# Regrouping batch 1's attention and moving its q^T to a DMA transpose in a fused attention and expert kernel

## The chip, the cores and the metric

The kernel runs on one core of a Trainium2 chip. The metric is device time in microseconds (us) of one execution. A profile records one execution with every instruction and every DMA packet; its times count from the start of the span, which is some 2 us shorter than the device time (330.9 and 332.65 us for the profiled run of the kernel before). Engines: PE is TensorE, PEld its weight loads, DVE is VectorE, ACT is ScalarE, POOL is GpSimd, SP is SyncE.

## The reference

Eight batches of attention with 8 heads, sequence 1024 and head size 64, in which k and v are first projected from 1024 to 64 positions; then a layer with two input matrices, a maximum and an output matrix.

```python
k_proj = einsum('ks,bhsd->bhkd', E, k);  v_proj = einsum('ks,bhsd->bhkd', F, v)
attn   = softmax(q @ k_proj^T / sqrt(64)) @ v_proj          # (8, 8, 1024, 64)
x      = attn, transposed and reshaped to (8192, 512)
out    = maximum(x @ w1, x @ w2) @ w_out                    # (8192, 512) float32
```

## The kernel before

The loads cast q, k and v of one batch to fp16, 1 MB each, and are issued by GpSimd. A batch has four attention "groups" (g, j): four heads g and half of the positions j. A group is a score step (TensorE, then exp on ScalarE), a sum step, a value step, and a multiply on VectorE. The projected k is transposed too; that tile is called kpt. The layer that follows works in 16 "units", two to a batch; each unit's products are cut into small pieces, between which the steps of later batches are put by hand. Unit (1, 0) needs only the groups with j = 0 of batch 1, unit (1, 1) those with j = 1.

The scores need q transposed. There are two ways to do it:

```python
def step_qt(t, h0, nh=2, i0=0, i1=NI, att=False):      # TensorE, then a copy by VectorE
    ...
            nc.tensor.transpose(out=qt_ps[...], in_=t["q"][:, h0 + h, ...], identity=ident16)
    nc.vector.tensor_copy(out=t["qt"][...], in_=qt_ps[...])

def step_qt_dma(t, h0=0, h1=H):                        # a DMA transpose, issued by SP
    nc.sync.dma_start_transpose(out=t["qt"][:, h0:h1]..., in_=t["q"][:, h0:h1]...)

def step_gate(t, n="kpt"):                             # GpSimd waits here until t[n] is written
    nc.gpsimd.tensor_copy(out=junk, in_=t[n][0:1, H - 1, 0:1])
```

GpSimd works in order, so a gate holds back all loads behind it. In the kernel before, batches 2 to 7 use the DMA transposes, with the next batch's loads behind a gate. Batch 1 transposes on TensorE, and all its four groups run within unit 0. Batch 2's k is loaded directly behind batch 1's q; its v and q follow as soon as batch 1's projection has freed their buffers.

The softmax here doesn't subtract the row's maximum and nothing guards it: scores larger than these inputs give would overflow.

Of the kernel before, what the change touches and what calls it, by code (L numbers as in the profile page):

```python
# [16 lines left out]
def kernel(  # L17
# [14 lines left out]
    B, H, S, D = q.shape  # L32
# [27 lines left out]
    def mm_bank(dtype=FP32, n=None):  # L60
        if n is None:
            n = turn.pop(0)
            turn.append(n)
        return ps.tile([128, 512 if dtype == FP32 else 1024], dtype, tag=f"mm{n}", name="mm_ps")

    def att_banks(dtype=FP32):
        return ps.tile(
            [128, 2, 512 if dtype == FP32 else 1024], dtype, tag="att", bufs=2, name="att_ps"
        )
# [6 lines left out]
            name=nc.get_next_instruction_name(),  # L76
# [17 lines left out]
    def alloc(t, n):  # L94
        t[n] = kvq.tile([128, H, NC, D], FP16, tag="kvq", name=f"{n}_sb")

    def load_all(t, b, n, src):
        alloc(t, n)
        load(t, n, src, b, 0, H)

    def load(t, n, src, b, h0, h1):
        nc.gpsimd.dma_start(  # L102
            out=t[n][:, h0:h1],
            in_=src[b, h0:h1].rearrange("h (p c) d -> p h c d", c=NC),
        )

    tiles = {b: {} for b in range(B)}
# [180 lines left out]
    def values_into(t, g, j, at_ps):  # L288
        for z in range(2):
            tiles_into(  # L290
                lambda o: at_ps[o][:, z * W : (z + 1) * W], t["ex", g, j],
                lambda rows, hh: t["vp"][rows, 4 * g + hh, z, :],
            )

    def new_xt(t):
        t["xt"] = xpool.tile([128, NP2, 2, HALF], FP16, tag="xt", name="xt_sb")

    def x_out(t, g, j):
        return t["xt"][:, 2 * g : 2 * g + 2, :, j * W : (j + 1) * W]
# [15 lines left out]
        ld = t["ld", g, j]  # L315
        nc.scalar.activation(out=ld, in_=ld, func=ACTF.Exp, scale=-1.0)

    def step_at(t, g, j):
        if "xt" not in t:
            new_xt(t)  # L320
        ld = t.pop(("ld", g, j))
        at_ps = [mm_bank() for _ in range(2)]
        values_into(t, g, j, at_ps)
        for o in range(2):
            nc.vector.tensor_tensor(  # L325
                out=x_out(t, g, j)[:, :, o, :],
                in0=at_ps[o].rearrange("q (z n) -> q z n", z=2),
                in1=ld[:, o, None, :].broadcast_to([128, 2, W]),
                op=ALU.mult,
            )  # L330
# [121 lines left out]
    U = {(b, o): {"n": n, "b": b, "o": o, "t": tiles[b]} for n, (b, o) in enumerate(units)}  # L452
# [260 lines left out]
    t = tiles[0]  # L713
# [25 lines left out]
    step_dn(t, 1, 0)  # L739
    step_inv(t, 1, 0)  # L740
    step_at(t, 0, 0)
    step_dn(t, 1, 1)
    step_inv(t, 0, 1)
    step_kv(t, 4, 8, "v")
    step_inv(t, 1, 1)
    step_at(t, 1, 0)
    step_wd(0)

# [6 lines left out]

    def loads(b, *names):
        for n in names:
            b_ = b + (n == "k" and b < 2)
            if b_ < B:
                load_all(tiles[b_], b_, n, {"k": k, "v": v, "q": q}[n])  # L760

    slots = [
        (0, u0[0]), (None, f(step_at, 0, 1)), (1, u0[1]), (None, f(step_at, 1, 1)),
        (None, lambda: loads(1, "v", "q", "k")),
        (None, wd[1]), (2, u1[0]), (3, u1[1]), (4, u0[2]), (None, wt[0]), (5, u0[3]),
        (None, wd[2]), (None, wt[1]), (6, u1[2]), (7, u1[3]), (8, u0[4]), (9, u0[5]), (None, wd[3]),
        (None, wt[2]), (10, u1[4]), (11, u1[5]), (12, u0[6]), (13, u0[7]), (None, wt[3]),
# [29 lines left out]
    def at_slot(key, s, *a):  # L797
        steps.setdefault(key, []).append(lambda: s(*a))
# [11 lines left out]
    t = tiles[1]  # L810
    at_slot((0, 19), new_attn, t)
    at_slot((0, 19), lambda: turn.__setitem__(slice(None), [2, 3]))
    for n, x in enumerate((
        "kv", "", "kpt", "qt00 qt10", "", "sc00 qt01 qt11", "sc10", "dn00 in00", "sc01",
        "at00 dn10 in10", "sc11", "at10 dn01 in01", "dn11 in11", "at01", "at11",
    )):
        key = ("P", 0, (n - 1) // 2, (n - 1) % 2) if n else (0, 19)
        for name in x.split():
            if name[0] == "k":
                if name == "kpt":  # L820
                    at_slot(key, step_kpt, t, 0, H, True)
                else:
                    at_slot(key, step_kv, t)
                    at_slot(key, loads, 2, "v", "q")
            else:
                g, j = int(name[2]), int(name[3])
                s_ = {"qt": step_qt, "sc": step_sc,
                      "dn": step_dn, "in": step_inv, "at": step_at}[name[:2]]
                at_slot(key, s_, t, *((4 * g, 4, 2 * j, 2 * j + 2) if name[:2] == "qt" else (g, j)))
        if n in (1, 5):  # L830
            at_slot(key, step_t, 1, (0, 1) if n == 1 else (2, 3))
        if 6 <= n < 10:
            at_slot(key, sums_x, U[0, 1], ((2, 0, 1, 3)[n - 6],))


    t = tiles[2]
    at_slot(("P", 0, 6, 0), new_attn, t)
    at_slot(("G", 1, 0), step_kv, t, 0, H, "kv", True)
    at_slot(("U", 1, 0, 1), step_kpt, t, 0, H, True)
    at_slot(("G", 1, 0), step_qt_dma, t, 0, H // 2)  # L840
    at_slot(("G", 1, 0), step_qt_dma, t, H // 2, H)
    at_slot(("U", 1, 0, 6), step_gate, t, "qt")
    at_slot(("U", 1, 0, 6), loads, 3, "k", "v", "q")

    for b in range(3, B):
        t = tiles[b]
        n = 2 * b - 3
# [3 lines left out]
        at_slot(("U", n, 0, 1), step_kv, t, 0, H, "kv", True, True)  # L851
        at_slot(("U", n, 0, 6), step_gate, t)
        at_slot(("U", n, 0, 6), loads, b + 1, "k", "v", "q")
    groups = [(tiles[b], g, j) for b in range(2, B) for j in range(2) for g in range(2)]
    none = (None, None, None)
    for i, (new, old) in enumerate(zip([*groups, none], [none, *groups])):
        n, h = divmod(i + 3, 2)
        if new[0] is not None:
            at_slot(("G", n, h), lambda t=new[0], h=h: t.__setitem__("first", (h, 1 - h)))
        at_slot(("G", n, h), step_group, *new, *old)  # L860
        at_slot(("U", n, h, 0), step_later)
        at_slot(("U", n, h, 2), step_later)
# [59 lines left out]
```

## Time and profile before

| | before |
|---|---|
| time, median of 4 runs in the rounds with the changed kernel | 333.76 us (332.14 to 333.92) |
| span of the profile | 330.9 us |
| TensorE busy | 97% |
| batch 1's projection starts | 51.3 us |
| batch 1's q landed | 52.7 us |
| batch 2's projection (needs k and v) starts | 71.6 us |
| batch 2's first scores (need half of q^T) start | 82.0 us |

TensorE has next to no idle time after 82 us (busy for 244.2 of the 248.9 us).

Two lines of the view by stretches show what the DMA engines give. The columns are the stretch, its length, busy time of the engines PE, PEld, DVE, ACT and POOL with numbers of instructions, granted clock of TensorE, DMA share, and GB/s that the DMA engines moved. In the first stretch only loads run, in the second loads and stores of results:

```profile
40.00:53.00 13.00, 13.00 (x75) 6.06 (x73) 12.45 (x22) 3.35 (x5) 0.00 (x0) 1.00 1.24 207
91.00:97.00 6.00, 6.00 (x57) 5.38 (x55) 4.89 (x9) 4.55 (x9) 0.00 (x0) 1.00 1.17 243
```

With loads alone the engines are busy throughout (their share is 1.24) and write 207 GB/s: 1 MB every 5 us.

### The profile page before, as it was taken

How to read it: one execution, taken by the hardware profiler on the slowest of the kernel's cores; microseconds unless marked ns; L12 is line 12 of the kernel's file. 1: busy time of each engine (PE TensorE's matmuls, PEld its weight loads, DVE VectorE, ACT ScalarE, POOL GpSimd, SP SyncE). 2: the span in 40 equal slices, each digit the busy share in tenths (PEclk: the TensorE clock that was granted, in tenths of full speed). 3: DMA queues.
4: the chain of work that ended last, by engine and by line, in shares of the span. 5: the costliest groups of instructions: out<-in, count | busy, mean ns of one | idle time of the engine just before them, and what ended most of it. 6: DMA issues, size and time to landing. Idle time of an engine off the chain costs nothing.

```text
span 330.9 us, 9012 instructions
## 1 busy us (share of the span) xinstructions
PE 319.5 (97%) x3852; PEld 247.9 (75%) x3852; DVE 239.9 (73%) x426; ACT 201.4 (61%) x358; POOL 37.1 (11%) x56
## 2 busy tenths in 40 slices
PE   8968999999999999999999999999999999999994
PEld 4532546658888788878888788878887888888883
DVE  1354698988677779677969878777967796969572
ACT  2452422744676677767777577667776777765541
POOL 8645002003000030003000110003000000000000
PEclk9997999999999999999999999999999999999998
DMA  8999999998994979995998799996999321212132
GB/s 161 205 199 204 202 207 196 207 189 149 197 239 125 185 96 218 200 218 90 198 238 197 118 155 239 205 180 98 219 201 198 76 96 34 97 34 95 35 128 96
DMA packets 74680, 53.14 MB, mean 161 GB/s; under 512 B 29456, under 2 KB 74512, under 8 KB 74640
## 3 DMA queue, kind: packets, MB, share of 16 engines
q0 software_dynamic: 29376, 28.31, 54.0%
q1 hardware_dynamic: 45264, 24.25, 30.6%
q8 instruction: 30, 0.49, 0.6%
q14 instruction: 10, 0.08, 0.1%
HBM read 57.15 MB, written 16.78 MB: 223 GB/s over the span
## 4 chain that ended last, share of the span: by engine, by line
PE 87%; DMA 5%; DVE 4%; issue 1%; POOL 1%; ACT 0%; DVEq 0%; POOLq 0%
PE mm_ps L632 43%; PE mm_ps L554 25%; PE mm_ps L400 5%; PE att_ps L180 3%; DMA big<-in_moe_w_dram 3%; PE att_ps L278 3%; PE mm_ps L266 3%; DMA k_sb<-in_k_dram 2%; PE mm_ps L436 2%; DVE xt_sb L325 1%; DVE o_sb L656 1%; PE mm_ps L278 1%; DVE gt_sb L569 1%; POOL k_sb L102 1%; PE mm_ps L237 1%
## 5 line engine op out<-in xcount | busy, mean ns | idle before, releaser
L525 ACT COPY p_sb<-mm_ps 128x512 f32<-128x512 f32 x172 | 97.1, 593 | 46.9 <-PE mm_ps L554 33.3
L632 PEld LDWEIGHTS <-big 128*128 128x128 f16 x768 | 73.4, 98 | 12.3 <-issue 3.7
L632 PE MATMUL mm_ps<-T_sb,big 128*128 128x256 f16 x576 | 78.1, 273 | 0.0
L569 DVE TENSOR_TENSOR gt_sb<-mm_ps,p_sb 128x512 f16<-128x512 f32 x56 | 38.5, 688 | 46.5 <-PE mm_ps L554 46.5
L554 PE MATMUL mm_ps<-big,big 128*128 128x256 f16 x336 | 50.4, 273 | 0.0
L554 PEld LDWEIGHTS <-big 128*128 128x128 f16 x448 | 43.8, 98 | 5.2
L632 PEld LDWEIGHTS <-gt_sb 128*128 128x128 f16 x384 | 35.6, 98 | 10.1 <-issue 5.8
L632 PE MATMUL mm_ps<-wo_sb,gt_sb 128*128 128x256 f16 x256 | 42.9, 273 | 0.1
L554 PEld LDWEIGHTS <-wd_sb 128*128 128x128 f16 x336 | 32.9, 98 | 4.2 <-issue 0.4
L554 PE MATMUL mm_ps<-xt_sb,wd_sb 128*128 128x256 f16 x224 | 33.6, 273 | 0.2 <-ACT ex_sb L351 0.2
L351 ACT ACTIVATE ex_sb<-mm_ps 128x512 f16<-128x512 f32 x48 | 26.1, 597 | 9.3 <-PE att_ps L278 7.0
L656 DVE TENSOR_TENSOR o_sb<-mm_ps,p_sb 128x512 f32<-128x512 f32 x32 | 21.9, 685 | 10.6 <-PE mm_ps L632 7.1
L377 DVE TENSOR_TENSOR xt_sb<-att_ps,ld_sb 128x1024 f16<-128x1024 f32 x24 | 29.3, 1219 | 0.1
L632 PE MATMUL mm_ps<-m_sb,xt_sb 128*128 128x256 f16 x128 | 24.4, 273 | 0.0
L604 ACT ACTIVATE gt_sb<-mm_ps 128x512 f16<-128x512 f32 x28 | 16.8, 600 | 8.7 <-PE mm_ps L554 8.7
L515 DVE TENSOR_TENSOR big<-gt_sb 128x1024 f16<-128x1024 f16 x32 | 21.9, 685 | 0.2
L572 DVE TENSOR_SCALAR gt_sb<-gt_sb 128x512 f16<-128x512 f16 (+1 forms) x56 | 20.4, 364 | 1.9
L632 PE MATMUL mm_ps<-T_sb,gt_sb 128*128 128x256 f16 x128 | 21.5, 273 | 0.0
L632 PE MATMUL mm_ps<-wo_sb,big 128*128 128x256 f16 x128 | 21.5, 273 | 0.0
L632 PEld LDWEIGHTS <-xt_sb 128*128 128x128 f16 x192 | 18.8, 98 | 2.2
L229 POOL COPY junk<-kpt_sb 1x1 f16<-1x1 f16 x5 | 0.9, 176 | 166.4 <-DMA kpt_sb<-kp_sb 166.4
L400 PE MATMUL mm_ps<-xt_sb,wd_sb 128*128 128x512 f16 x64 | 16.3, 401 | 3.0 <-DVE wd_sb L414 2.1
(86 smaller groups left out, 435.0 us busy)
## 6 DMA issues: line engine op xcount, KB each, us to landing
out_dram<-o_sb SPq DMA_DIRECT2D x63, 256.0 KB, 2.5
k_sb<-in_k_dram POOLq DMA_DIRECT2D x7, 1024.0 KB, 9.7
v_sb<-in_v_dram POOLq DMA_DIRECT2D x7, 1024.0 KB, 17.0
q_sb<-in_q_dram POOLq DMA_DIRECT2D x7, 1024.0 KB, 22.2
k_sb<-in_k_dram POOLq DMA_DIRECT2D x4, 256.0 KB, 6.4
q_sb<-in_q_dram POOLq DMA_DIRECT2D x4, 256.0 KB, 7.5
v_sb<-in_v_dram POOLq DMA_DIRECT2D x2, 512.0 KB, 12.0
big<-in_moe_w_dram POOLq DMA_DIRECT2D x8, 128.0 KB, 10.2
```

What stands on the lines that cost most here:

```text
L278: nc.tensor.matmul(out=dst(r ^ (hh % 2))[hh * Z : (hh + 1) * Z, :], lhsT=weights(rows, hh), rhs=ex[rows, hh % 2, hh // 2 * W : (hh // 2 + ...
L351: nc.scalar.activation(out=t["ex", g, j][:, e, :], in_=banks[e], func=ACTF.Exp, scale=scale)
L377: nc.vector.tensor_tensor(out=x_out(t, g, j).rearrange("q z o n -> q o z n"), in0=at_ps.rearrange("q o (z n) -> q o z n", z=2), in1=ld[:, ...
L400: nc.tensor.matmul(out=h_ps, lhsT=wd_sb[:, r, fb * 128 : (fb + 1) * 128], rhs=t["xt"][:, r, :, j * W : (j + 1) * W], start=(r == 0), stop= ...
L515: nc.vector.tensor_tensor(out=S(i), in0=x, in1=y, op=op)
L525: copy(out=x, in_=bank)
L554: nc.tensor.matmul(out=bank[:, m * W : (m + 1) * W], lhsT=w_[:, n_, (2 * d + m) * 128 : (2 * d + m + 1) * 128], rhs=a[:, n_, :], start=(n ...
L569: nc.vector.tensor_tensor(out=c_blk(j, c), in0=two(x), in1=two(y), op=ALU.add)
L572: nc.vector.tensor_scalar_max(ap, ap, 0.0)
L604: nc.scalar.activation(out=out, in_=in_, func=ACTF.Relu)
L632: nc.tensor.matmul(out=bank[:, i * CH : (i + 1) * CH], lhsT=a(c)[:, i * 128 : (i + 1) * 128], rhs=w_(c), start=(n is not None and m == (lo ...
L656: nc.vector.tensor_tensor(out=o_sb, in0=two(x), in1=two(y), op=ALU.add)
```

## The change

The intent: take the 32 transposes of batch 1's q and two of its four groups out of unit 0, where TensorE's stream is broken up most. q^T of batch 1 comes by DMA; batch 2's loads are gated behind it. As they come later, batch 2's projection, kpt and q^T are moved a few slots later. One value step (`AT10`) uses another pair of banks of PSUM, the memory that TensorE writes to (`att`). In the slot lists below, `qt` is a transposing step on TensorE, `sc` a score, `dn` a sum, `in` its inverse and `at` a value step; the two digits are g and j. The lines `...` are cuts.

```diff
-            b_ = b + (n == "k" and b < 2)
-            if b_ < B:
-                load_all(tiles[b_], b_, n, {"k": k, "v": v, "q": q}[n])
+            if b < B:
+                load_all(tiles[b], b, n, {"k": k, "v": v, "q": q}[n])
...
-        (None, lambda: loads(1, "v", "q", "k")),
+        (None, lambda: loads(1, "v", "q")),
...
-        "kv", "", "kpt", "qt00 qt10", "", "sc00 qt01 qt11", "sc10", "dn00 in00", "sc01",
-        "at00 dn10 in10", "sc11", "at10 dn01 in01", "dn11 in11", "at01", "at11",
+        "kv", "", "kpt", "", "", "", "", "sc00 sc10", "", "dn00 in00 dn10 in10", "", "",
+        "at00 AT10 sc01", "", "",
...
                     at_slot(key, step_kv, t)
-                    at_slot(key, loads, 2, "v", "q")
+                    at_slot(key, step_qt_dma, t, 0, H // 2)
+                    at_slot(key, step_qt_dma, t, H // 2, H)
+                    at_slot(key, step_gate, t, "qt")
+                    at_slot(key, loads, 2, "k", "v", "q")
...
-    at_slot(("G", 1, 0), step_kv, t, 0, H, "kv", True)
-    at_slot(("U", 1, 0, 1), step_kpt, t, 0, H, True)
-    at_slot(("G", 1, 0), step_qt_dma, t, 0, H // 2)
-    at_slot(("G", 1, 0), step_qt_dma, t, H // 2, H)
+    at_slot(("U", 1, 0, 1), step_kv, t, 0, H, "kv", True)
+    at_slot(("U", 1, 0, 4), step_kpt, t, 0, H, True)
+    at_slot(("U", 1, 0, 2), step_qt_dma, t, 0, H // 2)
+    at_slot(("U", 1, 0, 2), step_qt_dma, t, H // 2, H)
...
-    groups = [(tiles[b], g, j) for b in range(2, B) for j in range(2) for g in range(2)]
+    groups = [(tiles[b], g, j) for b in range(1, B) for j in range(2) for g in range(2)][2:]
...
```

More of the change, by code (lines that the diff above doesn't have):

```diff
@@ L316, in step_inv, with step_at @@
         nc.scalar.activation(out=ld, in_=ld, func=ACTF.Exp, scale=-1.0)
-    def step_at(t, g, j):
+    def step_at(t, g, j, att=False):
         if "xt" not in t:
@@ L321, in step_at @@
         ld = t.pop(("ld", g, j))
-        at_ps = [mm_bank() for _ in range(2)]
+        if att:
+            both = att_banks()
+            at_ps = [both[:, o, :] for o in range(2)]
+        else:
+            at_ps = [mm_bank() for _ in range(2)]
         values_into(t, g, j, at_ps)
@@ L823 @@
                     at_slot(key, step_kv, t)
-                    at_slot(key, loads, 2, "v", "q")
+                    at_slot(key, step_qt_dma, t, 0, H // 2)
+                    at_slot(key, step_qt_dma, t, H // 2, H)
+                    at_slot(key, step_gate, t, "qt")
+                    at_slot(key, loads, 2, "k", "v", "q")
             else:
                 g, j = int(name[2]), int(name[3])
-                s_ = {"qt": step_qt, "sc": step_sc,
-                      "dn": step_dn, "in": step_inv, "at": step_at}[name[:2]]
-                at_slot(key, s_, t, *((4 * g, 4, 2 * j, 2 * j + 2) if name[:2] == "qt" else (g, j)))
+                s_ = {"sc": step_sc,
+                      "dn": step_dn, "in": step_inv, "at": step_at, "AT": step_at}[name[:2]]
+                args = (4 * g, 4, 2 * j, 2 * j + 2) if name[:2] == "qt" else (g, j)
+                at_slot(key, s_, t, *args, *([True] if name[:2] == "AT" else []))
         if n in (1, 5):
@@ L853 @@
         at_slot(("U", n, 0, 6), loads, b + 1, "k", "v", "q")
-    groups = [(tiles[b], g, j) for b in range(2, B) for j in range(2) for g in range(2)]
+    groups = [(tiles[b], g, j) for b in range(1, B) for j in range(2) for g in range(2)][2:]
     none = (None, None, None)
-    for i, (new, old) in enumerate(zip([*groups, none], [none, *groups])):
-        n, h = divmod(i + 3, 2)
+    for i, (new, old) in enumerate(zip([*groups[1:], none], groups)):
+        n, h = divmod(i + 2, 2)
         if new[0] is not None:
```

## The prediction

> **What bounds the kernel now.** I began with the page, to see whether one engine carries the span (330.9 us), and then asked for the chain that ended last.
>
> ```profile
> PE 319.5 (97%) x3852; PEld 247.9 (75%) x3852; DVE 239.9 (73%) x426; ACT 201.4 (61%) x358; POOL 37.1 (11%) x56
> ...
> DMA  8999999998994979995998799996999321212132
> ...
> PE 87%; DMA 5%; DVE 4%; issue 1%; POOL 1%; ACT 0%; DVEq 0%; POOLq 0%
> ```
>
> TensorE is busy for 97% and makes 87% of the chain, so an instruction taken off it is time won, and a wait put in front of it is time lost. But the DMA engines also read 8 or 9 in most slices until three quarters of the span. So two resources are near their limit, and I have to follow both.
>
> The change acts between 53 and 82 us: unit 0's output products (from 53.16 us, after batch 1's projection of k and v), then the start of unit 1. I went through that stretch on TensorE's weight loads, whose starts show the true pace: the products follow each other at 0.109 us (4 in 0.44 us), and every switch to an attention step and back costs about 0.1 us more. One real stall stands at the end of unit 0:
>
> ```profile
> 68.12 0.33 PEld L632 LDWEIGHTS <-gt_sb 128*128 128x128 f16 x4 [0.20 <-issue]
> 68.46 0.21 PEld L632 LDWEIGHTS <-xt_sb 128*128 128x128 f16 x2
> 68.88 0.09 PEld L278 LDWEIGHTS <-vp_sb 64*32 64x32 f16 x1 [0.21 <-issue]
> 69.27 0.09 PEld L278 LDWEIGHTS <-vp_sb 64*32 64x32 f16 x1 [0.30 <-issue]
> 69.87 0.14 PEld L278 LDWEIGHTS <-vp_sb 64*32 64x32 f16 x14 [0.51 <-issue]
> 70.20 0.33 PEld L632 LDWEIGHTS <-gt_sb 128*128 128x128 f16 x4 [0.20 <-issue]
> ```
>
> The last value step (L278) needs two banks that VectorE's multiply still holds: 1.32 us for what takes 0.34 us elsewhere.
>
> The other resource, the queue of loads that GpSimd issues (timeline of POOL; columns: start, us, what):
>
> ```profile
> 27.69 0.89 POOL L102 DMA_DIRECT2D q_sb<-in_q_dram  x1
> 28.55 0.90 POOL L102 DMA_DIRECT2D k_sb<-in_k_dram  x1
> 53.53 0.88 POOL L102 DMA_DIRECT2D v_sb<-in_v_dram  x1 [24.07 <-PE mm_ps L180]
> 54.39 0.89 POOL L102 DMA_DIRECT2D q_sb<-in_q_dram  x1
> 78.03 0.26 POOL L229 COPY junk<-qt_sb 1x1 f16<-1x1 f16 x1 [22.75 <-DMA qt_sb<-q_sb]
> 78.55 0.88 POOL L102 DMA_DIRECT2D k_sb<-in_k_dram  x1 [0.25 <-issue]
> ```
>
> These are batch 1's q, batch 2's k, v and q, the gate on batch 2's q^T, and batch 3's k. The time from issue to landing, in the DMA views of short windows (first line of the windows 27.6 to 28.5, then 78 to 82, then 106 to 108):
>
> ```profile
> q_sb<-in_q_dram POOLq DMA_DIRECT2D x1, 1024.0 KB, 25.0
> ```
>
> ```profile
> k_sb<-in_k_dram POOLq DMA_DIRECT2D x1, 1024.0 KB, 9.6
> v_sb<-in_v_dram POOLq DMA_DIRECT2D x1, 1024.0 KB, 15.7
> q_sb<-in_q_dram POOLq DMA_DIRECT2D x1, 1024.0 KB, 21.6
> ```
>
> ```profile
> qt_sb<-q_sb SPq DMA_TRANSPOSE x1, 4.6
> ```
>
> So batch 1's q lands at 27.69 + 25.0 = 52.7 us. Batch 2's k lands at 28.55 + 29.1 = 57.7, its v at 53.53 + 9.8 = 63.3, its q at 54.39 + 14.9 = 69.3. TensorE asks for k and v at 71.6 and for batch 2's first scores, which need the first half of q^T, at 82.0:
>
> ```profile
> 82.00 0.41 PE L266 MATMUL mm_ps<-qt_sb,kpt_sb 64*32 64x256 f16 x16
> ```
>
> Both times nothing is waited for: the slack is 8 us for v and some 6 us for q^T (its first transfer starts at 70.09 and lands 5.5 us later). I expect the change to live or die by this slack.
>
> **What the Trainium skill says.** "TensorEngine Tiling (Array Packing)", section Key Properties, says that a change of tiling mode drains the engine; the trace agrees, with 0.76 us for six products beside an attention step against 6 x 0.109 = 0.655 alone. "DMA: Bandwidth & Descriptors", section Issuing engines are not separate DMA queues, says that transfers issued by different engines interleave on the same 16 DMA engines. The trace agrees: 200 GB/s moved by loads alone (86 to 90 us), and 243 GB/s by loads and stores together (91 to 97 us), so that loads give way to stores. The same page's Latency and other measured facts gives DMA transposes 261 GB/s; here 1 MB of them moves at 211 GB/s (108 to 112.5 us), and the measurement is what I use. "TensorE: Matmul & The Clock Gate", What's actually happening, puts the clock at half after an idle window of about 3.4 us; the trace has one such stretch, granted clock 0.50 from 25.0 to 28.4 us, after waits of 2 us and less around 20 to 25 us.
>
> **The change part by part, on TensorE.** Taken out: 32 transposes of batch 1's q in two runs that take 0.95 and 0.85 us, with their switches 2.0 us, and VectorE's 4 copies of them, 2.6 us, beside other work. Unit 0's products are 14 pieces x 0.655 = 9.2 us, and run from 53.16 to 70.20 = 17.0 us today, so attention and switches cost 7.8 us there. In the changed order only kpt (0.37), two scores together (0.6), two sums (0.35) and two values with one early score (0.8) stay, in four runs with 0.1 us each: 2.5 us. That is 5.3 us less in unit 0. Unit 1 gets the other two groups: one run of score, sums and values (0.67 + 0.1 us, as in the later units), and 24 matmuls more beside the score already there (0.33 us), 1.1 us in all. Without any new wait the change is worth 5.3 - 1.1 = 4.2 us, of which 1.0 us is the stall shown. TensorE would then reach batch 2's first score at 82.0 - 4.2 = 77.8 us. The rest of the program is the same in length.
>
> **The change on the DMA side.** Today batch 2's k stands in the queue directly behind batch 1's q, and v and q follow at 53.5. After the change all three wait for batch 1's q^T, which waits for batch 1's q:
> - q landed: 52.7 us (nothing ahead of it in the queue changes).
> - q^T, two transfers: later pairs take 7.7, 7.5 and 8.1 us from the first's start to the second's landing (106.50 + 2.4 + 5.3 and so on). The queue is empty here, so 7.5: 60.2 us. Batch 1's second score step then waits too, for about 2 us.
> - gate and issue: 78.03 to 78.55 today, 0.5: k issued at 60.7 us.
> - k, v, q: the three issued at 78.55, 79.42 and 80.28 landed 9.6, 16.6 and 23.3 us after the first issue, in company of 1 MB of stores. Here unit 0's last three stores and unit 1's first fall into the same stretch, so I keep these: k at 70.3, v at 77.3, q at 84.0.
> - TensorE reaches batch 2's projection at about 71.5 us, three slots later than before in its order (which is what the change's last part grants), and waits 5.8 us for v.
> - first half of q^T: 4.6 to 6.3 us after q; with 5.0, 89.0 us. TensorE would arrive at 77.3 + 1.85 (the projection) + 5.9 (what stands between) = 85.1, or 86.8 if the clock halves for a window after the wait; it waits again until 89.0.
>
> So the score that starts at 82.0 today starts at 89.0: plus 7.0 us, and TensorE, full from there on, cannot win it back. The three slots of delay are some 2 us, too few. Later loads: batch 3's go out at about 92 instead of 78.55, its v lands at 109 against a projection at 109.64 + 7, so the lateness ends there. 333.6 + 7.0 = 340.6; as the gate and the loads have more room to be quicker than slower (no stores while TensorE stands), I take 340.0.
>
> **Rivals.** (1) The gain comes through in full: 333.6 - 4.2 = 329.4. For it: the TensorE sum is firm. Against it: even with no store in the way, q lands at 84.0 - 3.3 = 80.7 us (four stores of 0.25 MB, each taking some 2.1 us in which loads move about 120 instead of 200 KB per us, by the rate of 91 to 97 us), and the score at 85. (2) The waits only eat the gain, 333 to 336: if the pair of transposes on an idle queue took 5 us (1 MB at 211 GB/s) and loads met few stores. (3) A blocked store queue: the q^T transfers of batch 2 stand in the same queue as the stores and wait there for q from about 78 to 84 us; with four output buffers that should not yet stop VectorE, but if it does, or a full half-clock window lies on the path, 342 to 344. (4) VectorE becomes the bound in unit 1: against it, 78% busy in later units that have two groups and no stall.
>
> **Range and chances.** 335 to 344 us holds rivals 2 and 3; the 2% line is at 340.3, almost my middle. Faster by over 2%: 0.02; within 2%: 0.52; slower by over 2%: 0.46.
>
> **What would show it.** Right: no q transposes on TensorE in unit 0; unit 0's products some 3 us shorter; GpSimd's gate at about 60 us and k issued right after; DMA nearly idle for loads from 53 to 62 us; TensorE waiting for v at 71 to 77 us and for q^T before batch 2's first score at about 89 us; the chain with more DMA and q_sb or v_sb in it. Wrong: batch 2's v landed before 72 us, or that score at 82 us or earlier, or new idle time on TensorE in later units.

## The result

The changed kernel takes 343.29 us (median of 4 runs, 341.36 to 345.68) against 333.76 us. The ratio is 1.03, with a 95% interval of 1.0227 to 1.0373. Ratios here are the mean time of one kernel's fast runs over that of the other's of the same rounds, so not quite the ratio of the medians. At the 2% line that is slower.

The page of the changed kernel, the lines that answer to those of before (busy time, PE, granted clock and DMA in 40 slices of 8.5 us, chain that ended last):

```profile
PE 321.2 (95%) x3820; PEld 248.4 (73%) x3820; DVE 237.3 (70%) x420; ACT 201.2 (59%) x359; POOL 37.5 (11%) x57
...
PE   8977999955999999999999999999999999999994
...
PEclk9997999995999999999999999999999999999999
DMA  7999998899699979999799959995998621202132
...
PE 72%; issue 11%; DMA 9%; POOL 4%; DVE 2%; ACT 0%; DVEq 0%; POOLq 0%
```

TensorE's row falls to 5 in two slices, from 68 to 85 us, and its granted clock to 5 in the slice from 76 us on. The chain, given in order of time (start, us, what), says what stands there:

```profile
28.74 31.99 issue
...
60.76 0.18 POOL junk L229
...
62.11 17.75 DMA v_sb<-in_v_dram
79.86 0.04 issue
79.90 3.57 PE att_ps L180 x15
```

The 32 us called "issue" are GpSimd standing at the gate; they are most of the 11% in the chain's summary. Then comes batch 2's v, for which TensorE waits, and then the projection itself, which takes 3.57 us instead of 1.85. The view of waits of TensorE has the same wait from its side (columns: who waited for what, us in total, times, longest):

```profile
PE att_ps L180 <- DMA v_sb<-in_v_dram: 7.6, 1, 7.6
```

GpSimd's timeline, which answers to the one in the prediction, and the times to landing of the first two loads behind the gate:

```profile
60.76 0.18 POOL L229 COPY junk<-qt_sb 1x1 f16<-1x1 f16 x1 [32.01 <-DMA qt_sb<-q_sb]
61.24 0.88 POOL L102 DMA_DIRECT2D k_sb<-in_k_dram  x1 [0.31 <-PE att_ps L266]
62.11 0.89 POOL L102 DMA_DIRECT2D v_sb<-in_v_dram  x1
62.97 0.90 POOL L102 DMA_DIRECT2D q_sb<-in_q_dram  x1
```

```profile
k_sb<-in_k_dram POOLq DMA_DIRECT2D x1, 1024.0 KB, 10.6
v_sb<-in_v_dram POOLq DMA_DIRECT2D x1, 1024.0 KB, 17.8
```

v lands at 62.11 + 17.8 = 79.9 us. In the kernel before it landed at 63.3. Two more stretches of the changed kernel show how the loads start and what the wait leaves behind:

```profile
62.00:69.00 7.00, 7.00 (x152) 5.41 (x149) 6.07 (x11) 4.75 (x8) 1.88 (x3) 1.00 0.96 131
79.80:83.50 3.70, 3.60 (x16) 1.61 (x16) 0.00 (x0) 0.00 (x0) 0.00 (x0) 0.50 1.20 202
```

In the first, the loads have just started from an idle queue and reach 131 GB/s on average, not the 207 of a queue that has been running. In the second TensorE projects k and v at a granted clock of 0.50. The Trainium skill, page "TensorE: Matmul & The Clock Gate", section What's actually happening, puts the clock at half after an idle window of about 3.4 us; this stretch, after 7.6 us of waiting, agrees. The half-clock stretch of the kernel before (25.0 to 28.4 us) came after waits of at most 2.1 us, so this does not show that one unbroken wait of that length is needed. Batch 2's first scores then start at 90.54 us (weight loads of TensorE) instead of 82.00:

```profile
90.54 0.23 PEld L266 LDWEIGHTS <-kpt_sb 64*32 64x32 f16 x16
```

That is 8.54 us later, and the spans differ by 339.6 - 330.9 = 8.7 us. From this moment on the two profiles are equally long (249.1 and 248.9 us), so the whole difference between them arises before it.

### The profile page after: what moved, and what is told of

Same layout as the page of the kernel before. It is cut to its first block, busy times and chain, and to the rows that moved or that the text cites. A ratio compares the mean times of both kernels' runs of the same rounds, so it can differ in the third digit from the quotient of the medians.

```text
span 339.6 us, 8944 instructions
## 1 busy us (share of the span) xinstructions
PE 321.2 (95%) x3820; PEld 248.4 (73%) x3820; DVE 237.3 (70%) x420; ACT 201.2 (59%) x359; POOL 37.5 (11%) x57
## 3 DMA queue, kind: packets, MB, share of 16 engines
q0 software_dynamic: 29376, 28.31, 52.7%
## 4 chain that ended last, share of the span: by engine, by line
PE 72%; issue 11%; DMA 9%; POOL 4%; DVE 2%; ACT 0%; DVEq 0%; POOLq 0%
PE mm_ps L636 39%; PE mm_ps L558 25%; DMA v_sb<-in_v_dram 9%; PE att_ps L180 4%; PE att_ps L278 3%; PE mm_ps L266 3%; POOL q_sb L102 1%; POOL big L126 1%; POOL k_sb L102 1%; DVE gt_sb L573 1%; DVE o_sb L660 1%; DVE xt_sb L381 0%; POOL v_sb L102 0%; POOL wo_sb L130 0%; ACT ex_sb L355 0%
## 5 line engine op out<-in xcount | busy, mean ns | idle before, releaser
L355 ACT ACTIVATE ex_sb<-mm_ps 128x512 f16<-128x512 f32 x50 | 27.2, 597 | 9.6 <-PE att_ps L278 7.0
L381 DVE TENSOR_TENSOR xt_sb<-att_ps,ld_sb 128x1024 f16<-128x1024 f32 x26 | 31.7, 1218 | 0.1
L180 PEld LDWEIGHTS <-eft 128*64 128x64 f16 x160 | 10.2, 118 | 16.4 <-issue 12.3
L180 PE MATMUL att_ps<-v_sb,eft 128*64 128x512 f16 x48 | 13.1, 423 | 7.6 <-DMA v_sb<-in_v_dram 7.6
```

The costliest lines, as they stand in the source:

```text
L180: nc.tensor.matmul(out=kv_ps[r * KP : (r + 1) * KP, 0:n], lhsT=eft[:, i, c, :], rhs=t[w][:, h0:h1, c, :], start=(c == 0), stop=(c == NC - 1),)
L355: nc.scalar.activation(out=t["ex", g, j][:, e, :], in_=banks[e], func=ACTF.Exp, scale=scale)
L381: nc.vector.tensor_tensor(out=x_out(t, g, j).rearrange("q z o n -> q o z n"), in0=at_ps.rearrange("q o (z n) -> q o z n", z=2), in1=ld[:, ...
```

## The experiments

All outputs are right. One run each of e2, e6, e7 and e11 was slow; the ratios leave these out, the medians do not. Theory 1: the time is set by when batch 2's v and q^T arrive, and they arrive late because batch 1's q^T takes its turn on the DMA engines first. Theory 2: the regrouping itself, two groups in unit 1, costs the time.

### e1: batch 2's k in front of the gate again

```diff
-        (None, lambda: loads(1, "v", "q")),
+        (None, lambda: loads(1, "v", "q", "k")),        # and loads() as in the kernel before
-                    at_slot(key, loads, 2, "k", "v", "q")
+                    at_slot(key, loads, 2, "v", "q")
```

> The changed kernel, but batch 2's k is loaded directly behind batch 1's q as before; only v and q stay behind the gate. Theory 1 (the lateness of batch 2's loads sets the time): k no longer takes its 5 us between the gate and v. It now shares the DMA engines with batch 1's q^T, so the gate opens some 2 us later (62 to 63 instead of 60.8 us); v lands at about 75 instead of 79.9, q at 80 instead of 85, batch 2's first scores start at about 86 instead of 90.5; time about 338.5 us (336.5 to 340.5). Theory 2 (two groups in unit 1, or the new order on TensorE, cost the time): no change, 342 to 345 us.

Measured: 339.95 us, ratio 1.0196 (1.0147 to 1.0244). As theory 1 has it, there is no wait for v any more and the first scores start at 85.95 us. But the gate opened only at 64.06 us, and TensorE waited for batch 1's q^T in unit 0. The view is TensorE's timeline, with the wait in brackets:

```profile
62.43 0.41 PE L266 MATMUL att_ps<-qt_sb,kpt_sb 64*32 64x256 f16 x16 [3.41 <-DMA qt_sb<-q_sb]
64.05 0.63 PE L266 MATMUL att_ps<-qt_sb,kpt_sb 64*32 64x256 f16 x16 [1.21 <-DMA qt_sb<-q_sb]
```

In this run one load beside the transposes was enough to make them late. A further wait that I had not foreseen stands at 121 us: batch 3's first scores wait 1.9 us for batch 3's transposed k.

### e3: the regrouping alone

The changed kernel with batch 1's q transposed on TensorE (`"kv", "", "kpt", "qt00 qt10", "", "qt01 qt11", "", "sc00 sc10", ...`), no q^T by DMA for batch 1, no gate, loads as before.

> The regrouping alone: two groups in unit 0 and two in unit 1, batch 2's steps at their new slots, but batch 1's q transposed on TensorE and all loads issued as in the kernel before (no gate). Theory 1: no wait for v or q^T; 32 transposes come back (2 us of the 4.2 us gain), so about 331.5 us (330.5 to 332.5), some 0.6% faster than before. Theory 2: slower than the kernel before, 335 us or more.

Measured: 331.37 us, ratio 0.9939 (0.9888 to 0.9989). The first scores of batch 2 start at 79.80 us instead of 82.00:

```profile
79.80 0.23 PEld L266 LDWEIGHTS <-kpt_sb 64*32 64x32 f16 x16
```

So the regrouping is worth 2.2 us with the transposes still on TensorE, as worked out (2.0 us if both profiles are counted from the start of batch 1's projection). Theory 2 falls.

### e4: the DMA part alone

The changed kernel with the four groups of batch 1 in unit 0, as before (the slot list with all `qt` entries taken out, and the old `groups` lines).

> The other part alone: batch 1's q^T by DMA with the gate and batch 2's steps three slots later, but all four groups of batch 1 in unit 0 as before. Theory 1: v lands at about 80 us whatever TensorE does, batch 2's first scores start at about 90.5 us, so the time is that of the changed kernel, 342 to 344.5 us. Theory 2: most of the loss goes away, 336 us or less.

Measured: 342.65 us, ratio 1.027 (1.021 to 1.033). The first scores start at 90.56 us, against 90.54 in the changed kernel. TensorE's order in unit 0 makes next to no difference to that moment; the DMA side sets it. That the two agree so closely is in part chance: the gate opened 1.1 us later here (61.84), and v then took 2 us less to land (15.8 after its issue). The wait for v is only 2.5 us here, as TensorE comes later, and the first scores waited 2.3 us for q^T.

### e5: batch 2's projection four unit steps later

```diff
-    at_slot(("U", 1, 0, 1), step_kv, t, 0, H, "kv", True)
-    at_slot(("U", 1, 0, 4), step_kpt, t, 0, H, True)
+    at_slot(("U", 1, 0, 5), step_kv, t, 0, H, "kv", True)
+    at_slot(("U", 1, 0, 6), step_kpt, t, 0, H, True)
```

> The changed kernel with batch 2's projection of k and v four unit steps later and its kpt two later, so that TensorE has some 3.5 us more to do before it needs v. If the wait for v (8 us) and the half clock after it are what costs, the time falls by 3 us or more, to 340 us or less. If q^T of batch 2 binds just as hard (first half landing at about 90.3 us), the first scores cannot start before 90.3 us and the time stays within 0.7 us of the changed kernel's, 342.5 to 344 us. I expect the second.

Measured: 342.42 us, ratio 1.0247 (1.0176 to 1.0319). The wait for v shrinks to 1.7 us and another takes its place (TensorE's timeline):

```profile
91.17 0.63 PE L266 MATMUL mm_ps<-qt_sb,kpt_sb 64*32 64x256 f16 x16 [6.24 <-DMA qt_sb<-q_sb]
```

So v and q^T bind at nearly the same moment, and moving slots cannot bring the time back. The gain of at most 0.9 us by the medians is within the spread of the two kernels; against the repeat of the changed kernel (e8, 342.64 us) it is 0.2.

### e2: no gate

The loads as before, no gate; one unused transpose of batch 1's q on TensorE keeps its buffer until later (by the order of the buffers, batch 2's v would otherwise take that of batch 1's q and wait for the transposes even without the gate; no run shows this).

> The changed kernel without the gate: batch 2's k, v and q are issued when they were before (k behind batch 1's q, v and q after batch 1's projection), beside batch 1's q^T by DMA. One small unused transpose of batch 1's q on TensorE in slot 6 keeps its buffer from being taken for batch 2's v, which would bring the wait back. If the gate alone is the cost: no wait left, 330 us or less. Theory 1 (there is not the DMA time for q^T at this place): the wait moves to q^T. With k alone beside it the two transfers took 10 us (first experiment); with v and q behind it I expect 11 to 14 us, so TensorE waits 5 to 8 us in unit 0, batch 2's first scores start at 84 to 87 us, and the time is 336 to 340 us.

Measured: 354.73 us (fast runs 350.4, 353.83 and 355.62), ratio 1.059 (1.0479 to 1.0701). The direction was right, the size far off: I expected 11 to 14 us for the two transposes. They landed 17.2 and 23.8 us after their issues, and TensorE waited 10.5 and 11.0 us for them, with its clock at 0.50 from 64 to 75 us. How the two queues shared the engines is told by their packets, here between 70 and 76 us, when loads (q0) and transposes (q1) both had work (columns: packets, MB, share of 16 engines):

```profile
q0 software_dynamic: 860, 0.86, 85.4%
q1 hardware_dynamic: 1004, 0.26, 37.2%
```

A load's packet holds 1 KB and a transpose's 256 bytes. So the transposes get 0.26 MB in 6 us, 43 GB/s, where alone (54 to 57 us of the changed kernel) they move 212. The Trainium skill, page "DMA: Bandwidth & Descriptors", section Queues, rings and completion order, says that each engine goes round between the queues with work, a packet at a time. In this window the counts are near each other, as that would have it; from 56 to 60 us, with v's load also under way, they are not (1316 packets of transposes, 176 of loads). So this run does not bear out equal turns, and whether the profile's packets are those that the page means is not shown. What it does show is that both lose: from 56 to 80 us the loads moved 2.20 MB and the queue of the transposes 1.06 MB, 136 GB/s together, where either alone moves over 200. Why is left open. In these runs the gate costs less than its absence.

### e7: half of q^T by DMA, beside the loads

The version of e3, with heads 4 to 7 by one DMA transpose without a gate, and their score three slots later.

> A version that may beat both: the regrouping with the loads as before (no gate), q^T of batch 1 half by TensorE (heads 0 to 3, 16 transposes) and half by DMA (heads 4 to 7, one transfer, beside the loads), with the score that needs the second half three slots later. It takes 1 us more off TensorE than the regrouping with all transposes on TensorE. If one transfer of half the size hides beside the loads: 330.4 us, 0.3% under that version. If the DMA engines have no room even for half: the score of heads 4 to 7 waits or v lands after 72 us, 332 to 336 us.

Measured: 341.44 us, ratio 1.0207 (1.0131 to 1.0284). One transfer of half the size took 19.2 us beside the loads, and the score waited 9.7 us for it. A miss (even the worse case expected 332 to 336 us), of the kind that e2 shows.

### e10: late loads without any DMA transpose of batch 1

The version of e3, but batch 2's three loads behind a gate on the q^T that TensorE and VectorE make.

```diff
+        if n == 4:
+            at_slot(key, step_gate, t, "qt")
+            at_slot(key, loads, 2, "k", "v", "q")
```

> The version with the regrouping and all transposes on TensorE (no q^T by DMA for batch 1 at all), but batch 2's k, v and q are held back by a gate on batch 1's q^T that TensorE and VectorE make, which opens at about 58.5 us instead of 60.8. It has the late loads and nothing else of the DMA part. If the late loads are the whole loss: k issued at about 59, v landing at 77, q at 83, batch 2's first scores at about 88 instead of 79.8 us, time 339.5 us (337.5 to 341). If the loss came from the DMA transposes themselves: 331.4 us, as without the gate.

Measured: 341.05 us, ratio 1.0262 (1.0227 to 1.0298), just above the range that I expected (to 341); its profiled run was its fastest (337.91 us). In it the gate opened at 56.92, TensorE waited 5.2 us for v, and the first scores started at 86.95 us:

```profile
86.95 0.23 PEld L266 LDWEIGHTS <-kpt_sb 64*32 64x32 f16 x16
```

Against e3, only the time of the loads differs: holding them back alone moves the first scores by 86.95 - 79.80 = 7.2 us in the profiles, and costs 341.05 - 331.85 = 9.2 us by the medians of these rounds (e9 below is e3 again). Nothing of it needs a DMA transpose of batch 1. The changed kernel is slower still by 1.6 to 2.2 us (342.64 and 343.29); there q^T by DMA opens the gate at 60.76, 3.8 us later than here. That this makes up the rest is likely, and was not tested alone.

### e6 and e11: the slack in the kernel before

> The kernel before with one thing changed: batch 2's k is issued after batch 1's projection, together with v and q, so v and q land about 5 us later (v about 69, q about 75 us). It measures the slack on which the prediction rests. If v has 8 us and q^T some 6 us of slack, nothing is waited for at 71.6 us and at most 1 us at 82 us: 333.6 us, within 1.5. If there is no slack, 338 us or more.

Measured: 333.92 us, ratio 0.9992 (0.993 to 1.0053). This shows nothing: the call was moved, but its buffer was free and nothing held GpSimd back, so the load still went out early (this profile was slow; I take only the order from it):

```profile
29.53 0.95 POOL L102 DMA_DIRECT2D k_sb<-in_k_dram  x1
```

Hence e11, with a gate on batch 1's projected k (its text calls this run the fifth; it was the sixth):

```diff
+                    at_slot(key, lambda: None if nc.gpsimd.tensor_copy(
+                        out=junk, in_=tiles[1]["kp"][0:1, H - 1, 0, 0:1]) else None)
+                    at_slot(key, loads, 2, "k", "v", "q")
```

> The slack once more, as the fifth experiment's edit did not move the load (GpSimd issued k at 29.5 us all the same, because its buffer is free). Here the kernel before holds batch 2's k, v and q back with a gate on batch 1's projected k, which opens at about 54 us: k issued at 54.5, v landing at about 69, q at about 75, first half of q^T at about 80.5 us against scores at 82.0. If the slack is what I took it for: 333.6 us, within 1.5. If it is smaller, TensorE waits at 71.6 or 82 us and the time is 335 us or more.

Measured: 336.94 us, of which 333.77, 336.93 and 336.96 are fast, ratio 1.008 (1.0034 to 1.0127). Outside what I expected. Its profiled run was slow, so I take only the order of events from it: q landed at 56.29 + 22.1 = 78.4 us, 9 us later than before instead of the 5 to 6 I reckoned with; the projection did not wait for v; the first scores waited 1.1 us for q^T, and two later batches' scores waited 3.5 us for their transposed k. So the slack is about 8 us for q as well: a delay of 9 us leaves a wait of 1.1. The prediction had 8 us for v and some 6 for q^T; its 6 was counted from a transfer that started at 70.09 us, 0.8 after q had landed, and took 5.5 us to land instead of the 4.5 here. The later waits are of the kind seen at 121 us in e1.

### e8 and e9: repeats

> The changed kernel once more, for a second profile. Its profiled run was its fastest (341.4 of 341.4 to 345.7 us). The second and fourth experiments showed a third wait, 2.3 us for batch 3's transposed k before batch 3's first scores at about 121 to 126 us, behind batch 3's q^T in the same queue; the first profile of the changed kernel has none of it. If the spread of its times comes from there, this profile, if of a run of 343 us or more, shows that wait of 1 to 4 us; the median stays 342 to 344.5 us.

Measured: 342.64 us, ratio 1.029 (1.0239 to 1.034). The runs meant by "second and fourth" are e1 and e4 (1.9 us each in TensorE's waits). The profiled run, 342.44 us, was not one of the 343 us or more that the expectation asks for, yet it has the wait that the first profile lacked:

```profile
PE mm_ps L266 <- DMA kpt_sb<-kp_sb: 1.5, 1, 1.5
```

The transfer of batch 3's transposed k landed 4.5 us after its issue, against 3.1 in the first profile and 2.7 in the kernel before. It stands in SP's queue behind batch 3's q^T and one store. Those were issued 5.8 us ahead of it here and 7.4 us ahead in the kernel before, as batch 3's loads went out at 93 instead of 78.6 us. In the kernel before, the scores come right after this transfer, so any further delay is a wait. A wait of this kind (0.9 us, after 200 us) also stands in the profile of e9, whose loads are not late. Why it took 4.5 us in one run and 3.1 in another, with almost the same times of issue, is not settled.

> The regrouping with all transposes on TensorE and the loads as before, once more with more rounds, as it is the only version that was faster than the kernel before: 331.4 us, ratio 0.994 with an interval that stays below 1.

Measured: 331.85 us (6 runs) against 332.98 us (11 runs), ratio 0.996 (0.9931 to 0.9989). The regrouping with all transposes on TensorE beats the kernel before by about half a per cent, and the changed kernel by about 3.

## Why the prediction was right

It gave 340.0 us with a range of 335 to 344, and 343.29 was measured: inside, near the slow end. Of the three outcomes it held "within 2%" the likeliest (0.52) and gave 0.46 to "slower", which came. By its own steps:

| step | predicted | profile of the changed kernel |
|---|---|---|
| batch 1's q landed | 52.7 us | the transposes that wait for it start at 52.65 |
| both halves of q^T landed, gate | 60.2 | 60.76 |
| k issued | 60.7 | 61.24 |
| v landed | 77.3 | 79.9 |
| q landed | 84.0 | 62.97 + 22.5 = 85.5 |
| TensorE reaches the projection | 71.5 | 71.86 (second profile, e8: 72.21) |
| wait for v | 5.8 | 7.6 |
| first half of batch 2's q^T landed | 89.0 | 85.56 + 4.4 = 90.0 |
| TensorE could start batch 2's first scores | 85.1 to 86.8 | 90.54 |
| batch 2's first scores | 89.0 | 90.54 |

- The gain on TensorE, 4.2 us without a new wait, was right: unit 0's products run from 53.17 to 70.21 us before and from 54.41 to 67.02 after, 4.4 us less with 0.6 us of new waits among them (5.3 predicted without any), and the added work in unit 1 takes 1.0 us (1.1 predicted). e3 gets 2.2 us of it. The wait for batch 1's q^T, predicted at about 2 us, was 0.4 us in the first profile, in which batch 1's projection began 1.24 us later than before, and 1.8 us in the second.
- The mechanism was right. The late loads are the loss: e4 has it without the regrouping, and e10 has most of it without batch 1's DMA transposes.
- The mis-sized term of the sum is "the three issued at 78.55, 79.42 and 80.28 landed 9.6, 16.6 and 23.3 us after the first issue ... so I keep these". From the first issue at 61.24 they landed after 10.6, 18.7 and 24.3 us. I thought that the loads had more room to be quicker than slower; they were 1 to 2 us slower. The slow start is not the reason: the loads from which I took the sizes also began on an idle queue, at 142 GB/s from 79.3 to 86.3 us against 131 here. The stores came earlier. In the 7 us after that, first in the kernel before (86.3 to 93.3), then in the changed one (69 to 76; q0 are the loads, q1 the stores):

```profile
q0 software_dynamic: 1177, 1.18, 103.4%
q1 hardware_dynamic: 331, 0.32, 16.8%
```

```profile
q0 software_dynamic: 893, 0.90, 78.0%
q1 hardware_dynamic: 731, 0.72, 37.6%
```

  Up to the landing of v the stores moved 1.05 MB in the changed kernel and 0.55 in the other; 0.5 MB at some 235 GB/s is an estimated 2.1 us, and v was 2.1 us late. The prediction had the right amount of stores for all three loads, but not that they would fall before v.
- The wait for q^T was predicted to be the one that counts at the end. This sign did not come: neither profile of the changed kernel has a wait for q^T before batch 2's first scores. In the first, its first half landed at 90.0 us and TensorE came at 90.54, later than the 85.1 to 86.8 predicted, because v landed 2.6 us later, the projection took 3.5 us at half clock instead of 1.85, and what follows took 7.1 us instead of 5.9. That the start was predicted only 1.5 us too early is thus in part luck: the path of TensorE, not that of q^T, came last. e4 and e5, which wait 2.3 and 6.2 us for q^T, show that q^T alone would have set about the same end.
- "Its v lands at 109 against a projection at 109.64 + 7, so the lateness ends there" holds for v, but not for everything: batch 3's transposed k, in the queue behind a late q^T, makes a third wait of 1.5 us in the second profile. The prediction did not look at that transfer. Of the 3.3 us between 340.0 and the measured median, 8.54 - 6.4 = 2.1 us are in the start of batch 2's first scores (340.0 stood for a shift of 6.4 us). The profiled run itself took 341.36 us, 1.9 us under its median; that of the kernel before, 332.65 us, was 1.1 under its own. So the shift of 8.54 us leaves 1.0 of the 9.5 us between the medians; the third wait, absent from the first profile and present in the second, is a part of this that was seen, and the rest is not explained.
- Rival 1 (the gain comes through) was rightly refused, and so was rival 2, which needed few stores. Rival 3 came true in part: the half-clock stretch lies on the path; that blocked stores stop VectorE is not seen (from 58 to 100 us it waits only for ScalarE and TensorE). VectorE did not become the bound (rival 4): from 83.4 to 118 us it is busy for 74% and TensorE for 99%.

## What to carry to other kernels

When a change moves work from a full engine to the DMA engines, follow the data that stands behind it in the queue up to the moment at which the full engine needs it: here 4 us of TensorE's time were paid for with 16 us in the arrival of the next batch's data (q at 85.5 instead of 69.3 us), of which only some 8 us were slack. Moving the consumer a few slots later helped here only until the next transfer in the row bound (e5). The DMA transposes did badly beside the bulk loads (17 to 24 us to land in e2 and e7, against about 5 alone), so here they needed their own place in time, and there was none that did not make the next loads late; on TensorE the transposes were cheaper (e3).

## What the Trainium skill lacked or had wrong

- "DMA: Bandwidth & Descriptors", Rules for kernel authors, says that a transpose next to ordinary DMAs needs nothing. It speaks there of correct results, and all runs were correct. What it lacks is the time: beside loads, the two transposes landed 17.2 and 23.8 us after their issues (e2), where two alone landed a median of 5.3 us after theirs (changed kernel), and loads and transposes together moved 136 GB/s from 56 to 80 us.
- The same page, Latency and other measured facts, gives DMA transposes 261 GB/s, measured on one kernel. Alone, from 54 to 57 us of the changed kernel, they moved 212.
- No page that I read has the slow start of casting loads after the queue was empty: 131 GB/s from 62 to 69 us of the changed kernel and 142 from 79.3 to 86.3 us of the kernel before, against 207 for loads in a running queue.
